# Three narrow chunks beside attention instead of five, with two attention steps to each d_ff tile from step 25

## The chip, the core and the metric

The kernel runs on one core of one Trainium2 chip. The metric is the device time of one execution in microseconds (us); lower is better. The profile is one execution on the same core, and its times are counted from the first instruction.

## What is computed

```python
def _attn_ref(q, k, v, omega):              # q, k, v: (4, 8, 576, 64); omega: (128, 64)
    scale = 1.0 / np.sqrt(np.sqrt(D))
    q_s, k_s = q * scale, k * scale
    def phi(x):
        proj = np.einsum('bhsd,md->bhsm', x, omega)
        h = proj - np.sum(x * x, axis=-1, keepdims=True) / 2.0
        return np.exp(h - np.max(h, axis=-1, keepdims=True)) / np.sqrt(m)
    q_p, k_p = phi(q_s), phi(k_s)
    kv = np.einsum('bhsm,bhsd->bhmd', k_p, v)
    z = np.sum(k_p, axis=2)
    num = np.einsum('bhsm,bhmd->bhsd', q_p, kv)
    den = np.einsum('bhsm,bhm->bhs', q_p, z)[..., None] + 1e-06
    return num / den

x = attention output as 2304 tokens x 512
h = x @ w_in                                # layer one: d_ff 2048
x = (np.maximum(h, 0) + alpha * np.minimum(h, 0)) @ w_out
out = ((x @ w_a) * (x @ w_b)) @ w_out2      # layer two: d_ff 1536
```

All values are fp32. Every fp32 product of the two layers is made of three faster ones: each operand is split into a high and a low part (`xh`/`xl`, `gh`/`gl`, and the two halves of a weight tile `w`), and high x high, high x low and low x high are summed.

## The kernel before

There are four stages. TensorE (PE) runs one fixed order of instructions; so does each other engine. Instructions stand in each engine's queue in the order in which the Python code issues them.

**Attention** goes in steps `s`, one token tile of one unit (a pair of heads, `u`) each. A step projects keys and queries (`pp(u, t)`, `a_proj`), takes the maxima (`nm`, VectorE, `a_max`) and exponentials (`ph`, ScalarE, up to 16 for two steps, `a_exp`). Later steps use the results: `kv` sums keys by values (`a_kv`), `tp` transposes the query features and copies them to `phT` (`a_t`; on ScalarE or VectorE, whichever the code counts as less loaded), `nd` multiplies by the kv state `kvp` and normalises (`rc`, `xn`, three VectorE instructions, `a_num`), and `xp` transposes the result into `xT` (`a_x`). `pp`, `tp`, `nd`, `xp` and the layer's input product `h` share one ring of five PSUM banks here, each reused after its readers are done.

**Layer one beside attention.** Layer one works by chunks of tokens and d_ff tiles `f`. A tile of a chunk is one input product `h` (12 matmuls), the activation (`u`, then a scalar-tensor-tensor, `gh`, `gl`) and one output product `y` (12 matmuls) that runs a while after it. A narrow chunk has 256 tokens. The first two narrow chunks go in two halves of the eight tiles; the first half's sums are parked in `xT` and added later (`xT<-y,xT`). Up to a point (`ALONE` pieces of `work0`) `A.run` takes one attention step with each tile. Behind it the `while` loop calls `group`, which takes two attention steps with two tiles, and leaves a group without tiles unless two are ready. In `group` the queue order is: `xp`, `kv`, `nd`, `nd`, `kv`, the late halves of the activation (`A.flush`), two projections with maxima and exponentials, x splits (`spread`), decoder work (`D_.go(5)`), `tp`, `y`, `tp`, `y`, then the `h` of the tiles.

**The decoder** unpacks weight tiles: `z` and `a` on GpSimd, `r` and `w` on ScalarE, a scalar-tensor-tensor `a`, an `ISA` instruction `a` on VectorE, and the low half of `w` on GpSimd or VectorE. It is paid by credit: `D_.step` gives it, 1 for a step and 2 for a group. There are 17 slots for tiles until attention is over.

**Layer one alone** works with wide chunks of 512 tokens (`Mlp.run`, class `Mlp` again), in two passes over d_ff: tiles 0 to 7 for all tokens that attention did not cover, then tiles 8 to 15 for all. `over` opens its buffers and splits the first inputs; `Mlp.open` takes its PSUM banks, four for outputs (`psy`) and four for inputs (`psh`). **Layer two** follows (`dual`, `back`) and is untouched.

The numbers that the change touches, before: `NCI = 5` narrow chunks, `REST = (512, 512)` wide ones in the first pass, `ALONE = 4` pieces run one step to a tile (16 tiles, steps 15 to 30).

Of the kernel before, what the change touches and what calls it, by code (L numbers as in the profile page):

```python
# [15 lines left out]
PSUM = bass.MemoryType.PSUM  # L16
# [7 lines left out]
KT = DM // P  # L24
# [8 lines left out]
WARM = 11  # L33
Q_LAG = 6
CI = 256
NCI = 5
NF0 = 8
NFH = 5
CB = 512
REST = (512, 512)  # L40
CHUNKS = (512, 512, 256, 512, 512)
NS = 25
NS1 = 17
# [9 lines left out]
DEC1 = 1.0  # L53
# [5 lines left out]
PACE2 = 1  # L59
PACE3 = 1  # L60
FIRST = 32
ALONE = 4
LAND = 5.0
SIDE = 0

# [2 lines left out]
def tile_kernel(ctx: ExitStack, tc: tile.TileContext, qT, kT, v1, omT, wbits, alpha, out):  # L68
# [37 lines left out]
    def place(q):  # L106

        if q < 20:
            return q
        if q < PB:  # L110
            return q if q < NS else q - NS
        return RING[(q - PB) % len(RING)]
# [14 lines left out]
    for ph in range(PH2):  # L127
        q = PB + QS * ph
        for j in range(2):
            f = 4 * ph + 2 * j  # L130
# [10 lines left out]
    def pick(*ways):  # L141

        def worst(w):
            return max(load[e] + w.get(e, 0.0) for e in load)

        i = min(range(len(ways)), key=lambda i: worst(ways[i]))
        for e, x in ways[i].items():
            load[e] += x
        return i
# [65 lines left out]
    class Decoder:  # L215
# [132 lines left out]
        def open(self, q):  # L348
            return place(q) in slots and (before[q] is None or self.free.get(before[q], False))
# [104 lines left out]
        def more(self, n):  # L454

            for _ in range(n):
                if self.advance() is not True:
                    return
# [11 lines left out]
    D_ = Decoder()  # L470
# [9 lines left out]
    class Mlp:  # L480
# [24 lines left out]
            self.banks = lambda h=None: self.open(pool, ybufs, h)  # L505

        def open(self, pool, ybufs, h):
            self.psy = pool(name=f"psy{self.cap}", bufs=ybufs, space=PSUM)
            self.psh, self.htag = h or (pool(name=f"psh{self.cap}", bufs=4, space=PSUM), "h")

        def split(self, ph, o, n, k):
            if (ph, o, k) in self.xs:
# [6 lines left out]

            way = pick({"dve": 1.2 * n / 1000}, *([] if self.pair or o == CI * NCI else [{"pool": 2.5 * n / 1000}]))  # L520
            (nc.vector, nc.gpsimd)[way].tensor_tensor(out=lo, in0=src, in1=hi.bitcast(F32), op=ALU.subtract)  # L521
# [466 lines left out]
    A = Mlp(st_m, CI, 2)  # L988
# [26 lines left out]
    with st_m:  # L1015
        A.banks((psp[0], "ps"))
        nxt_s = [SPLIT_AT]
        due = [0.0]

        def attn_next(high=None, low=None):  # L1020
            s = nxt_s[0]
            nxt_s[0] += 1
            D_.step(DEC1)
            pj = attn_1(s)
            if high:
                high()
            if pj:
                nm = a_max(*pj)
            loads(s)
            if low:  # L1030
                low()
            if pj:
                a_exp(*pj, nm)
            attn_2(s)
            A.after.append(lambda: attn_3(s))

        def attn_more():
            attn_next()
            A.flush()

        def inside(high, low):
            due[0] += 1.0
            if due[0] > 0 and nxt_s[0] < steps:
                due[0] -= 1.0
                attn_next(high, low)
            else:
                high()
                low()

        A.beside = inside  # L1050

        wait = {}

        def group(fronts, at):

            s = nxt_s[0]
            nxt_s[0] += 2
            D_.step(2 * DEC1)
            full = s < last_q
            todo = {n: wait[n][:2] for n in wait}  # L1060
            for n in wait:
                wait[n] = wait[n][2:]
            kv, t = list(todo["kv"]), list(todo["t"])
            for ut in todo["x"]:
                a_x(*ut)
            if kv:
                a_kv(*kv.pop(0))
            for ut in todo["num"]:
                a_num(*ut)
                wait["x"].append(ut)  # L1070
            if kv:
                a_kv(*kv.pop(0))
            spread(fronts, KT)
            A.flush()
            for x in (s, s + 1):
                pj = attn_1(x)
                loads(x)
                if pj:
                    a_exp(*pj, a_max(*pj))
                if x in ev["k"]:  # L1080
                    wait["kv"].append(ev["k"][x])
                if x in ev["q"]:
                    wait["t"].append(ev["q"][x])
            spread(line[at:at + 5], 2)
            D_.go(5)
            for i in range(2):
                if i < len(t):
                    a_t(*t[i])
                    wait["num"].append(t[i])
                if full:  # L1090
                    A.back_one(fronts, 2 - i)
            for w in fronts:
                A.whole(*w)
                if not full:
                    A.back_one(fronts)
            D_.go(3)

        def more():
            return nxt_s[0] < last_q or any(wait.values())

        def x_there(end, k, soon=False):
            b, t = divmod(end - 1, S)
            ut = (b * HG + k // 2, t // P)
            return ut in done["x"] or soon and ut in wait["x"][:2]

        def over():
            st_a.close()
            mlp_x.append(Mlp(st_u, CB, 4, RIGHT))
            for k in range(2):
                mlp_x[0].split(0, CI * NCI, CB, k)  # L1110


        work0 = [(0, CI * i, CI, fs, False) for fs in (range(NFH), range(NFH, NF0)) for i in range(2)]
        work0 += [(0, CI * i, CI, range(NF0), False) for i in range(2, NCI)]

        def ready(end, k):
            b, t = divmod(end - 1, S)
            while nxt_s[0] <= x_step[b * HG + k // 2, t // P]:
                due[0] -= 1
                attn_more()  # L1120

        def beside(ph, ci, i):
            A.flush()
            todo = [f for w in work0[ci:ci + 2] for f in w[3]]
            need = [2 * f for f in todo[i + 1:i + 2]] + [2 * todo[j] + 1 for j in (i - 1,) if j >= 0]
            while not all(q in D_.made for q in need) and nxt_s[0] < steps:
                due[0] -= 1
                attn_more()

        A.run(work0, beside, ready, stop=ALONE)  # L1130
        A.flush()
        started = [i for i in sorted(ev["k"]) if i < nxt_s[0]]
        wait.update({
            "kv": [ev["k"][i] for i in started if ev["k"][i] not in done["kv"]],
            "t": [ut for ut in queries if ut in phiq],
            "num": [ut for ut in queries if ut in phT],
            "x": [ut for ut in queries if ut in xns]})

        line = [(ph, o, n, f, lc) for ph, o, n, fs, lc in work0 for f in fs]

        def spread(fronts, most):

            todo = []
            for w in fronts:
                if w[:3] not in todo:
                    todo.append(w[:3])
            for ph, o, n in todo:
                for k in range(KT):
                    if most and (ph, o, k) not in A.xs and x_there(o + n, k):
                        A.split(ph, o, n, k)  # L1150
                        most -= 1

        i = sum(len(w[3]) for w in work0[:ALONE])
        while i < len(line):
            if not more():
                spread(line[i:i + 5], 2)
            pair = []
            early = 1 if more() else 0
            for w in line[i:i + 2]:
                ph, o, n, f, _ = w  # L1160
                if all((ph, o, k) in A.xs or x_there(o + n, k, True) for k in range(KT)) and D_.ready >= 2 * f + 2 - early:
                    pair.append(w)
            if len(pair) < 2 and more():
                pair = []
            if more():
                group(pair, i)
            else:
                for w in pair:
                    A.flush()
                    A.whole(*w)  # L1170
                    A.back_one(pair, 3)
                    D_.fill()
            i += len(pair)
        A.flush()
        while more():
            group([], i)
        over()
        while A.q:
            A.pop()
# [71 lines left out]
    with st_u:  # L1251
# [6 lines left out]
        work = []  # L1258
        for ph, fs, chunks in ((0, range(NF0), (CI,) * NCI + REST), (1, range(NF0, FA), CHUNKS)):
            work += [(ph, sum(chunks[:i]), n, fs, i == len(chunks) - 1)  # L1260
                     for i, n in enumerate(chunks) if ph or i >= NCI]

        def beside(ph, ci, i):
            D_.fetch()
            rate = RATE_A if ph == 0 else RATE_A2 if ci == len(REST) else RATE_X
            D_.step(rate * work[ci][2] / 384)
# [251 lines left out]
```

## Time and profile before

| what | value |
|---|---|
| median of 3 runs | 941.66 us (941.63 to 943.17) |
| the profiled execution's own time | 941.1 us |
| its span, first to last instruction | 939.3 us |
| TensorE matmul busy | 927.0 us, 99% |
| VectorE busy | 610.1 us, 65% |
| ScalarE busy | 508.9 us, 54% |
| GpSimd busy | 126.1 us, 13% |
| mean granted TensorE clock | 0.999 |

A timeline row gives the start, the length, the engine, the line, the operation with output and inputs, the shape and the count of merged instructions; in brackets how long the engine stood idle before it and who ended that. Instructions on one engine overlap by some tenths of a microsecond, so the distance from one start to the next is the better price of one. A busy engine says nothing of what it may be short of; the list of waits says who stood still for whom.

### The profile page before, as it was taken

What the parts mean: (1) busy time and instruction counts of PE and PEld (TensorE: products, weight loads), DVE (VectorE), ACT (ScalarE), POOL (GpSimd) and SP (SyncE); (2) the same over time, 40 slices, a digit from 0 to 9 for tenths busy, and PEclk for the clock granted to TensorE, in tenths of its full rate; (3) what the DMA queues carried; (4) which work ended last, traced back from release to release, by engine and by line L of the source; (5) the groups of instructions that cost most, each with busy time, mean ns of one, the idle gap of its engine ahead of it and who ended that gap; (6) DMA issues with size and microseconds to landing.
All of it is one profiled execution on the core that took longest, in us unless ns stands there. A gap on an engine that the chain in (4) does not pass through costs nothing.

```text
span 939.3 us, 16686 instructions
## 1 busy us (share of the span) xinstructions
PE 927.0 (99%) x6483; PEld 841.1 (90%) x6483; DVE 610.1 (65%) x1247; ACT 508.9 (54%) x1196; POOL 126.1 (13%) x107
## 2 busy tenths in 40 slices
PE   8899999999999999999999999999999999999998
PEld 7789999999888888889888999999999898989896
DVE  5987775644667677678676796866486833374633
ACT  7878766553455554455444555655456542444541
POOL 3677700000020201000000000000011111010201
PEclk9999999999999999999999999999999999999999
DMA  9454431000234342455555856169727368333323
GB/s 339 150 184 145 149 103 50 24 1 24 90 90 135 90 157 68 168 191 200 202 180 214 314 206 231 73 225 395 282 65 238 69 185 275 100 42 94 55 47 68
DMA packets 49566, 138.92 MB, mean 148 GB/s; under 512 B 4560, under 2 KB 11088, under 8 KB 49488
## 3 DMA queue, kind: packets, MB, share of 16 engines
q1 hardware_dynamic: 44592, 129.08, 38.6%
q0 software_dynamic: 4752, 8.65, 6.3%
q8 instruction: 51, 0.84, 0.4%
q14 instruction: 27, 0.22, 0.1%
q10 hardware_dynamic: 144, 0.13, 0.0%
HBM read 90.66 MB, written 47.19 MB: 147 GB/s over the span
## 4 chain that ended last, share of the span: by engine, by line
PE 94%; ACT 3%; DVE 2%; issue 0%; ACTq 0%
PE y L191 21%; PE h L191 21%; PE W L191 16%; PE o L191 16%; PE E L191 8%; PE B L191 4%; ACT ph L818 2%; PE tp L191 2%; PE kv L191 1%; PE nd L191 1%; PE xp L191 1%; DVE xl L521 0%; PE warm L191 0%; ACT r L259 0%; ACT phT L852 0%
## 5 line engine op out<-in xcount | busy, mean ns | idle before, releaser
L191 PE MATMUL h<-xh,w 128*128 128x256 f32 (+1 forms) x768 | 189.2, 338 | 1.1 <-DVE yo L191 0.7
L191 PE MATMUL y<-gh,w 128*128 128x256 f32 (+1 forms) x768 | 184.7, 339 | 0.0
L191 PEld LDWEIGHTS h<-xh,w 128*128 128x128 f32 x768 | 125.8, 190 | 16.8 <-DVE yo L191 0.9
L191 PEld LDWEIGHTS y<-gh,w 128*128 128x128 f32 x768 | 123.3, 189 | 15.0
L191 PE MATMUL o<-w,gh 128*128 128x512 f32 x432 | 133.2, 389 | 0.0
L191 PE MATMUL h<-xl,w 128*128 128x512 f32 (+1 forms) x384 | 109.9, 336 | 0.4 <-DVE xl L521 0.4
L191 PE MATMUL y<-gl,w 128*128 128x512 f32 (+1 forms) x384 | 109.5, 336 | 0.0
L191 PEld LDWEIGHTS o<-w,gh 128*128 128x128 f32 x432 | 81.0, 188 | 16.5
L191 DVE SCALAR_TENSOR_TENSOR h<-u,bend,h 128x512 f32<-128x512 f32 (+1 forms) x72 | 47.8, 664 | 56.5 <-ACT u L555 56.5
L191 PE MATMUL o<-w,gl 128*128 128x512 f32 x216 | 84.2, 390 | 0.0
L1417 POOL DMA_DIRECT2D out<-op x30 | 26.3, 875 | 421.9 <-ACT op L166 339.5
L567 ACT ACTIVATE gh<-h 128x512 fp32r<-128x512 f32 (+1 forms) x72 | 37.9, 527 | 64.3 <-DVE h L191 64.3
L191 PEld LDWEIGHTS h<-xl,w 128*128 128x128 f32 x384 | 64.4, 190 | 8.2 <-DVE xl L521 0.6
L191 PEld LDWEIGHTS y<-gl,w 128*128 128x128 f32 x384 | 64.1, 189 | 7.5
L555 ACT ACTIVATE u<-h 128x512 f32<-128x512 f32 (+1 forms) x72 | 38.0, 528 | 56.0 <-PE h L191 52.0
L521 POOL TENSOR_TENSOR xl<-xT,xh 128x512 fp32r<-128x512 f32 (+1 forms) x16 | 20.2, 1274 | 335.4 <-ACT xh L517 335.4
L166 ACT ACTIVATE u<-W 128x384 f32<-128x384 f32 x72 | 35.3, 492 | 50.6 <-PE W L191 46.8
L166 ACT ACTIVATE op<-o 128x512 f32<-128x512 f32 x51 | 30.4, 596 | 57.9 <-PE o L191 44.8
L191 DVE TENSOR_TENSOR u<-E,u 128x384 f32<-128x384 f32 x36 | 19.6, 555 | 52.5 <-PE E L191 49.7
L191 DVE TENSOR_TENSOR gl<-h,gh 128x512 fp32r<-128x512 f32 (+1 forms) x72 | 43.1, 598 | 15.4 <-ACT gh L567 14.6
L191 DVE CUSTOM_DVE_ANT_0 a<-a,r 128x1024 uint16<-128x1024 uint16 x68 | 48.9, 719 | 5.2 <-ACT r L259 1.2
L191 PEld LDWEIGHTS o<-w,gl 128*128 128x128 f32 x216 | 40.5, 188 | 8.4
(496 smaller groups left out, 1968.0 us busy)
## 6 DMA issues: line engine op xcount, KB each, us to landing
raw<-in_w SPq DMA_DIRECT2D x68, 512.0 KB, 4.8
w<-store SPq DMA_DIRECT2D x45, 512.0 KB, 6.7
store<-t_None SPq DMA_DIRECT2D x40, 512.0 KB, 3.6
st<-ypart SPq DMA_DIRECT2D x14, 768.0 KB, 7.7
out<-op POOLq DMA_DIRECT2D x30, 256.0 KB, 5.6
q<-in_qT SPq DMA_DIRECT2D x8, 576.0 KB, 4.1
v<-in_v SPq DMA_DIRECT2D x7, 650.0 KB, 5.6
yp<-ypart SPq DMA_DIRECT2D x4, 1024.0 KB, 5.8
```

The lines of the kernel that those rows point to most:

```text
L166: nc.scalar.activation(out, in_, AF.Copy)
L191: return call(*a, **k)
L521: (nc.vector, nc.gpsimd)[way].tensor_tensor(out=lo, in0=src, in1=hi.bitcast(F32), op=ALU.subtract)
L555: nc.scalar.activation(u_, hp, AF.Relu, scale=-1.0)
L567: nc.scalar.activation(gh, hp, AF.Copy)
L818: nc.scalar.activation(ph[:, 2 * pr + j], pair[j][:, o + pr], AF.Exp, bias=nm[:, j, o + pr:o + pr + 1])
L1417: nc.gpsimd.dma_start(out=dst, in_=op, accum_op=ALU.add)
```

## The change

- `NCI` 5 to 3 and `REST` from two to three wide chunks: tokens 768 to 1279 leave the narrow part and become one wide chunk.
- `ALONE` 4 to 2: one attention step with one tile ends after 10 tiles (steps 15 to 24). From step 25 on `group` runs.
- `group` now takes one tile, not two, with its two steps, one `y` at most between them, and the decoder gets 1 of credit for a group, not 2.
- `open` takes the input banks `psh` first, the output banks `psy` after them.
- `over` splits all four input quarters of the first wide chunk, not two.

```diff
-NCI = 5
+NCI = 3
-REST = (512, 512)
+REST = (512, 512, 512)
-ALONE = 4
+ALONE = 2
...
         def open(self, pool, ybufs, h):
+            self.psh, self.htag = h or (pool(name=f"psh{self.cap}", bufs=4, space=PSUM), "h")
             self.psy = pool(name=f"psy{self.cap}", bufs=ybufs, space=PSUM)
-            self.psh, self.htag = h or (pool(name=f"psh{self.cap}", bufs=4, space=PSUM), "h")
...
-            D_.step(2 * DEC1)
+            D_.step(DEC1)
...
                 if full:
-                    A.back_one(fronts, 2 - i)
+                    A.back_one(fronts, 1)
...
-            for k in range(2):
+            for k in range(KT):
                 mlp_x[0].split(0, CI * NCI, CB, k)
...
-            for w in line[i:i + 2]:
+            for w in line[i:i + 1] if more() else line[i:i + 2]:
...
-            if len(pair) < 2 and more():
-                pair = []
```

Three places show what this moves. The names are those of the steps above; the last number of a tile is the build's own and means nothing.

First place: TensorE at step 25, before.

```order
L191 MATMUL xp_2_1851<-ident,xn_2_1732 128x128 x2
L191 MATMUL h_0_5_1855<-xh_0_0_683,w_88 128x256
...
L191 MATMUL pp(5, 0)_False_1873<-xT,k_1381 128x128
...
L191 MATMUL kv_1505<-v_1070,ph_4_1792 64x65 x8
L191 MATMUL nd_4_1917<-kvp_170,phT_4_1837 64x65 x4
L191 MATMUL tp_2_1929<-ident,ph_2_1693 128x128 x4
...
L191 MATMUL xp_3_1948<-ident,xn_3_1830 128x128 x2
```

The same place on TensorE after the change:

```order
L191 MATMUL xp_2_1851<-ident,xn_2_1732 128x128 x2
L191 MATMUL xp_3_1855<-ident,xn_3_1830 128x128 x2
L191 MATMUL kv_1505<-v_1070,ph_4_1792 64x65 x8
L191 MATMUL nd_4_1868<-kvp_170,phT_4_1837 64x65 x4
L191 MATMUL pp(5, 0)_False_1878<-xT,k_1381 128x128
...
L191 MATMUL pp(5, 1)_False_1901<-xT,k_1381 128x128
```

The transpose `xp_3`, which stood behind `h`, `pp`, `kv`, `nd`, `tp` and a `y`, now stands directly behind `xp_2`.

Second place: ScalarE in the group of steps 29 and 30 of the changed kernel, from the second step's last exponentials.

```order
L818 ACTIVATE ph_0_2236<-pp(6, 0)_False_2222,nm(0, 6, 0)_2233 128x128 x2
L818 ACTIVATE ph_2_2237<-pp(6, 0)_False_2222,nm(0, 6, 0)_2233 128x128 x2
L517 ACTIVATE xh_512_0_2246<-xT 128x256
L517 ACTIVATE xh_512_1_2250<-xT 128x256
L259 ACTIVATE r_2258<-raw_2094 128x512
L308 ACTIVATE w_94<-a_2100 128x512
L852 ACTIVATE phT_1_2271<-tp_1_2266 128x512
L852 ACTIVATE phT_0_2290<-tp_0_2285 128x512
L587 ACTIVATE u_0_7_2305<-h_0_7_2292 128x256
L838 ACTIVATE kvp_170<-kv_1997 128x260
```

Before, `w_94` stood in step 27 on ScalarE, behind one step's exponentials and with no split ahead of it:

```order
L818 ACTIVATE ph_2_2091<-pp(5, 2)_False_2075,nm(0, 5, 2)_2085 128x128 x2
L818 ACTIVATE ph_1_2092<-pp(5, 2)_False_2075,nm(0, 5, 2)_2085 128x128 x2
L259 ACTIVATE r_2105<-raw_1995 128x512
L308 ACTIVATE w_94<-a_2001 128x512
L852 ACTIVATE phT_4_2138<-tp_4_2135 128x256
L894 ACTIVATE xT<-xp_2_2154 128x2x128
```

The last decoder tile now stands behind two steps' exponentials and two x splits, and both `phT` copies of the group stand behind it.

Third place: VectorE in the same group and the next of the changed kernel.

```order
L521 TENSOR_TENSOR xl_512_0_2247<-xT,xh_512_0_2246 128x256
L521 TENSOR_TENSOR xl_512_1_2251<-xT,xh_512_1_2250 128x256
L191 SCALAR_TENSOR_TENSOR a_2100<-z_2096,a_2100 128x512
L191 ISA a_2100<-a_2100,r_2098 128x1024
L191 SCALAR_TENSOR_TENSOR u_0_7_2305<-u_0_7_2305,bend,h_0_7_2292 128x256
...
L521 TENSOR_TENSOR xl_512_3_2416<-xT,xh_512_3_2415 128x256
L191 TENSOR_TENSOR xT<-y_0_0_2111,xT 128x256 x2
L191 TENSOR_TENSOR xT<-y_0_1_2112,xT 128x256 x2
L191 COPY phT_2_2448<-tp_2_2443 128x512
```

The decoder's `a` stands behind both `xl`, which read what ScalarE splits; one group on, `phT_2` stands behind two `xl` and four additions of the parked sums.

## Rows read from the trace of the kernel before

**Rows 1.** The page: busy time, share of the span, instructions of each engine.
```profile
PE 927.0 (99%) x6483; PEld 841.1 (90%) x6483; DVE 610.1 (65%) x1247; ACT 508.9 (54%) x1196; POOL 126.1 (13%) x107
```
**Rows 2.** Waits of TensorE: waiting <- waited for: us in total, times, longest.
```profile
PE h L191 <- DVE yo L191: 0.7, 1, 0.7
PE tp L191 <- DVE xn L191: 0.2, 1, 0.2
```
**Rows 3.** Chain of waits: start, us, engine and output, matmuls; narrow, then wide.
```profile
138.44 2.88 PE h L191 x24
...
252.51 2.72 PE h L191 x12
```
**Rows 4.** Timeline, TensorE: first transposes of steps 25, 31 and 39.
```profile
97.44 0.38 PE L191 MATMUL xp<-ident,xn 128*128 128x128 f32 x2
...
131.12 0.60 PE L191 MATMUL xp<-ident,xn 128*128 128x128 f32 x4
...
173.32 0.60 PE L191 MATMUL xp<-ident,xn 128*128 128x128 f32 x4
```
**Rows 5.** Timeline, all engines, at the end of the narrow chunks.
```profile
236.16 1.12 PE L191 MATMUL y<-gh,w 128*128 128x256 f32 x8
...
237.80 0.43 DVE L191 TENSOR_TENSOR gl<-u,gh 128x256 fp32r<-128x256 f32 x1 [0.48 <-ACT gh L594]
238.32 1.29 DVE L521 TENSOR_TENSOR xl<-xT,xh 128x512 fp32r<-128x512 f32 x2
...
241.33 0.50 PE L191 MATMUL h<-xh,w 128*128 128x512 f32 x1 [0.70 <-DVE yo L191]
```
**Rows 6.** Timeline, VectorE: the normalisation of step 24.
```profile
98.20 0.42 DVE L191 TENSOR_TENSOR xn<-nd,rc 128x256 f32<-128x256 f32 x1
```
**Rows 7.** Timeline, all engines: the group of steps 37 and 38.
```profile
163.11 0.48 DVE L191 SCALAR_TENSOR_TENSOR u<-u,bend,h 128x256 f32<-128x256 f32 x1 [0.96 <-ACT u L587]
...
165.87 0.61 PE L191 MATMUL pp(7, 3)_False<-xT,k 64*128 64x128 f32 x8
166.22 1.28 DVE L191 TENSOR_REDUCE nm(0, 7, 2)_3008<-pp(7, 2)_False 128x4 f32<-128x512 f32 x2
...
166.94 2.17 ACT L818 ACTIVATE ph<-pp(7, 2)_False,nm(0, 7, 2)_3008 128x128 f32<-128x128 f32 x8 [2.89 <-DVE nm(0, 7, 2)_3008 L191]
...
168.95 2.22 ACT L818 ACTIVATE ph<-pp(7, 3)_False,nm(0, 7, 3)_3031 128x128 f32<-128x128 f32 x8
...
170.94 0.83 ACT L517 ACTIVATE xh<-xT 128x256 fp32r<-128x256 f32 x2
...
171.50 0.76 DVE L521 TENSOR_TENSOR xl<-xT,xh 128x256 fp32r<-128x256 f32 x2 [2.81 <-ACT xh L517]
171.56 0.98 ACT L852 ACTIVATE phT<-tp 128x256 f32<-128x256 f32 x2
...
174.36 0.81 PE L191 MATMUL nd<-kvp,phT 128*64 128x65 f32 x22
```
**Rows 8.** Timeline, VectorE and ScalarE: decoder work and phT in single steps.
```profile
113.31 0.68 DVE L191 SCALAR_TENSOR_TENSOR a<-z,a 128x512 uint32<-128x512 uint32 x1
...
114.03 0.69 DVE L191 CUSTOM_DVE_ANT_0 a<-a,r 128x1024 uint16<-128x1024 uint16 x1
...
114.51 0.72 ACT L259 ACTIVATE r<-raw 128x512 uint32<-128x512 uint32 x1
...
115.07 0.68 ACT L308 ACTIVATE w<-a 128x512 fp32r<-128x512 f32 x1
...
115.59 0.43 ACT L852 ACTIVATE phT<-tp 128x256 f32<-128x256 f32 x1
```
**Rows 9.** Groups of instructions by shape, 97 to 131 us: additions of parked sums, decoder.
```profile
L191 DVE SCALAR_TENSOR_TENSOR a<-z,a 128x512 uint32<-128x512 uint32 x4 | 3.7, 930 | 0.0
...
L191 DVE TENSOR_TENSOR xT<-y,xT 128x256 f32<-128x256 f32 x4 | 1.4, 416 | 0.6 <-PE y L191 0.6
```
**Rows 10.** Windows: TensorE's busy time, instructions, granted clock, DMA share, GB/s.
```profile
18.00:20.00 2.00, 0.84 (x14) 1.00 1.08 404
```

## The prediction

> **What bounds the kernel now.** I read the page's busy times first: TensorE is busy for 927.0 of 939.3 us, every other engine at most 65% [rows 1]. A share that high is no proof, so next the waits of TensorE: beside the first 40 us there is one of 0.7 us where the wide chunks begin and one of 0.2 us in the grouped steps [rows 2]. So TensorE runs almost without a pause, and what the change is worth is the TensorE work that it takes away, less the pauses that it makes. For the first I read the chain, for the second the timelines of one group, of single steps and of the end of the narrow part.
>
> The profiled execution took 941.1 us, 0.6 under the median of the runs; the sum is made against 941.1. A measurement here can tell about 0.2% (1.9 us) from no change.
>
> **TensorE work taken away.** 512 tokens leave the narrow part. Two narrow products of 12 matmuls take 2.88 us, one wide one 2.72 [rows 3]. Eight tiles, each with an input and an output product: 16 x 0.16 = **2.6 us** less.
>
> Six steps (25 to 30) change from single steps to groups. From the transposes at 97.44 to those at 131.12 lie six single steps, 5.61 us each; less one `h` and one `y` (2.88) the attention in one is 2.73. From there to 173.32 lie four groups, 10.55 each; less two `h` and two `y` (5.76), halved, 2.39 [rows 3, 4]. 6 x 0.34 = **2.0 us** less: the same matmuls, with fewer changes between kinds. Steps differ a little in size, so 1.2 to 2.5.
>
> At the first wide product the wait of 0.7 us for `yo` goes [rows 2, 5]: with `psh` opened first, the banks that `yo` empties go to the outputs, needed three tiles later. What is late next? Only one `y` now lies between the last `h` and the last `y`. In the row before, the last `h` ends at 236.16 and `gl` at 238.23; with one `y` (1.44) in between, the late half is due near 238.56, its high half near 237.6, so at most 0.2 us is given back. The four splits follow `gl` at 0.65 each (1.29 for two [rows 5]) and end near 240.9; the fourth is due 2.2 us after 239.1, so it is hidden. Together **0.5 us** less.
>
> Gain: 2.6 + 2.0 + 0.5 = **5.1 us**. The rest of the kernel has the same work in the same order on TensorE; decoder work still ahead when attention ends is the same too (17 tiles made), with a wide chunk more to hide it.
>
> **Pauses that it makes.** A group keeps its two steps and loses one `h` and one `y`, its cover. I take the group at 162 to 173 us as a model, count from the end of the first projection (165.87) and subtract 2.88. TensorE reaches the next `xp` at 173.32, so 7.45 after, now **4.6**; the second `xp` 0.25 later, **4.8**; the first `nd` 1.04 after the first `xp` (174.36), now **5.6** [rows 4, 7].
>
> ScalarE must finish by then. From the maximum's start to the first exponential is 0.72; sixteen exponentials take 4.23 (166.94 to 171.17), fourteen about 3.7; the following operation starts 0.23 before the last one ends [rows 7]. With VectorE free the maxima start at about 0.1, so sixteen end at E = 5.05. The second `xp` takes the bank that the last exponentials leave, so it waits until E.
>
> I name the groups by steps and go through the seven heavy ones.
> - **25, 26.** `xp_3` stands right behind `xp_2`, due 97.6; its `xn` ended at 98.62 [rows 6], behind the decoder's operations of step 24, which stay where they are. Pause **1.1**.
> - **27, 28** (16 exponentials). E is past 4.8: 0.3. Behind the exponentials on ScalarE stand `r`, `w` (0.56 and 0.52 from start to start), then two `phT` (0.43 for half a tile, and 0.98 for half and whole) [rows 7, 8]. The first `phT` ends at E + 1.3 = 6.3, where `nd` is due at 5.9: 0.45; the second adds 0.25. Sum **1.0**.
> - **29, 30** (14). ScalarE's `u` stood behind `phT`, so VectorE gets to it late: scalar-tensor-tensor, copies, two normalisations and `gl` lie between it and the maxima, 3.1 us with two `gl` [rows 7], 2.7 with one. So the maxima start at 1.3 and E is 5.7; TensorE loses 0.9 to the banks. Now a chain through two engines: two `xh`, two `xl` (1.32 from the first `xh` to the last `xl` [rows 7]), scalar-tensor-tensor and `ISA` (1.4), `w` (0.6), `phT` (0.6) [rows 7, 8]. It starts at E - 0.23 and ends near 9.4; `nd` is due at 6.5: 2.9. The second `nd` needs the second `phT`, `u` and `kvp` behind it on ScalarE, three copies of some 0.45: 0.6 more. Sum **4.4**.
> - **31, 32** (14). Two `xh`, two `xl`, then four additions of the parked sums (1.4 [rows 9]) stand ahead of one `phT` on VectorE (0.6): done 3.1 after E, with `nd` due 1.3 after E and the first `nd` 0.1 late: 1.7; 0.4 for a bank. Sum **2.1**.
> - **33 to 38.** No decoder and no split: 0.6 (a bank, VectorE still behind), 0, and 0.5 for the sixteen of 37 and 38. Sum **1.1**. Groups after that have at most ten exponentials and pause no more than now.
>
> Pauses: 1.1 + 1.0 + 4.4 + 2.1 + 1.1 = **9.7 us**. Bounds: if VectorE is on time in each group, 6.8 remain (1.1, 0.9, 3.1, 1.5, 0.2); if the decoder's VectorE operation takes its mean of 0.93 [rows 9] rather than 0.68 and the delays add up, about 12.5. I take the middle, which follows the queues one group after another.
>
> DMA loads: keys, queries and values are issued in the same steps as before, now some 8 us for two steps rather than 11, still at least two steps ahead of their use; I cost them at nothing, and a late one would be seen as a wait of `pp` or `kv` for DMA.
>
> Sum: 941.1 - 5.1 + 9.7 = 945.7; the runs' median lay 0.6 above the profiled execution, so I take half of that: **946.0 us**, 0.46% above the median. With the bounds of pauses and gain 942.8 to 948.8.
>
> **The clock.** In the window 18 to 20 us TensorE was busy 0.84 of 2.00 us and the granted clock was 1.00 [rows 10]; by that row the pauses cost only their length. The Trainium skill ("TensorE: Matmul & The Clock Gate", section "HAM oscillation — how this bites in real kernels") says that idle gaps between bursts of matmuls make the gate throttle the array again, so that the next burst starts cold. By that rule the sum would be some 950; by the row it is 946. No single pause of the trace before is as long as the 2.9 us that I expect, so the row bears on it only in part.
>
> **Rivals.**
> - *The pauses stay under the gain: faster.* Place: the group of steps 29 and 30. If ScalarE and VectorE run ahead there, so that the exponentials end a good 2 us earlier than I put them, only step 25's 1.1 us, and some 1.5 elsewhere, remain. It decides where the pauses sum to less than 5.1 - 1.9 = 3.2. Then 941.1 - 5.1 + 2.6 = 938.6. For it: the grouped steps before paused 0.2 us in all. Against: the order of the queues, which no speed of VectorE shortens, since `phT` there stands behind seven operations that follow one another.
> - *Pauses and gain about equal.* The low bound of the pauses with the full gain gives 942.8; a little less, 941.7.
> - *The clock falls in a pause of steps 29 to 32.* 1.2 GHz instead of 2.4 doubles the matmuls; a group's TensorE work is some 7.8 us, and if half of one runs so, 4 us more: 950.
> - *The change doesn't do what it says* (groups that go without a tile). The order shows one tile in every group up to the last, so I give it nothing.
>
> **Chances.** Forecast 0.64; faster 0.09; equal 0.16; clock 0.11. The range leaves out the faster case and the far end of the clock case and takes in the bounds: 942.4 to 949.8. Within 0.2% (939.8 to 943.5) lie the equal case and the low edge of the forecast, less some of each: 0.16. Slower by over that 0.75, faster 0.09.
>
> **What would show it.** Right: waits of `xp` for VectorE near 98 us, of `nd` for ScalarE's `phT` between 110 and 140 us, the longest near 3 us; TensorE's narrow part over at about 203 us (before 241); the first wide `h` without a wait for `yo`; granted clock 1.00. Wrong: no `nd` wait over 1 us in that stretch; or waits for DMA; or a granted clock under 0.95 there; or new pauses in the wide part, which I hold to be none.

## The result and the profile after

The change makes the kernel slower: 948.03 us median of six runs (947.06 to 950.72) against 942.45 for the kernel before beside it (941.63 to 943.77). The ratio is 1.0071, 95% interval 1.0061 to 1.0081. The profiled execution took 949.5 us, its span 947.5.

The page of the changed kernel, busy times of the engines, against [rows 1]:

```profile
PE 928.4 (98%) x6291; PEld 832.3 (88%) x6291; DVE 605.9 (64%) x1220; ACT 506.1 (53%) x1173; POOL 133.5 (14%) x113
```

192 matmuls fewer (two narrow ones became one wide one), and yet TensorE is busy for 1.4 us longer, where the prediction took 4.6 us of its work away. So pauses need not be all of it: some of its work may have become slower.

Waits of TensorE from 97 to 206 us, the narrow part from step 25 on; before there were two, of 0.7 and 0.2 us [rows 2]:

```profile
PE nd L191 <- ACT phT L852: 2.8, 2, 2.5
PE nd L191 <- DVE phT L191: 1.3, 1, 1.3
PE xp L191 <- DVE xn L191: 0.9, 1, 0.9
PE xp L191 <- ACT ph L818: 0.4, 2, 0.3
PE nd L191 <- ACT kvp L838: 0.4, 1, 0.4
PE tp L191 <- DVE xn L191: 0.2, 1, 0.2
```

The timeline of TensorE shows where they stand (start, duration, operation, count, in brackets the idle time ahead and what ended it), with the first wide product as last row:

```profile
100.11 0.44 PE L191 MATMUL xp<-ident,xn 128*128 128x128 f32 x2 [0.86 <-DVE xn L191]
...
118.18 1.17 PE L191 MATMUL nd<-kvp,phT 128*64 128x65 f32 x24 [0.29 <-ACT phT L852]
...
126.17 0.44 PE L191 MATMUL xp<-ident,xn 128*128 128x128 f32 x2 [0.25 <-ACT ph L818]
...
129.74 0.69 PE L191 MATMUL nd<-kvp,phT 128*64 128x65 f32 x16 [2.52 <-ACT phT L852]
130.78 1.14 PE L191 MATMUL nd<-kvp,phT 128*64 128x65 f32 x16 [0.35 <-ACT kvp L838]
...
132.71 1.23 PE L191 MATMUL pp(6, 1)_False<-xT,k 64*128 64x128 f32 x8
...
142.22 0.69 PE L191 MATMUL nd<-kvp,phT 128*64 128x65 f32 x16 [1.34 <-DVE phT L191]
...
205.43 0.40 PE L191 MATMUL h<-xh,w 128*128 128x512 f32 x1
```

The waits come in the order and at the places that the prediction gave, the longest (2.52 us) for the `phT` that steps 29 and 30 make, which TensorE needs in the next group, ahead of the projections of steps 31 and 32. The first wide `h` waits for no `yo`, where before it did [rows 5]. The eight matmuls of `pp(6, 1)` at 132.71 take 1.23 us; eight such take 0.61 at full clock [rows 7]. The windows around them (length, TensorE's busy time, instructions, granted clock, DMA share, GB/s):

```profile
126.00:129.00 3.00, 1.05 (x18) 1.00 0.24 42
129.00:130.00 1.00, 0.26 (x8) 1.00 0.97 390
130.00:131.00 1.00, 0.65 (x20) 0.88 0.41 166
131.00:134.00 3.00, 3.00 (x44) 0.50 0.00 0
134.00:135.00 1.00, 1.00 (x20) 0.91 0.00 0
```

After 2.5 us without a matmul and another wait soon behind them, the clock goes from 2.4 to 1.2 GHz for some 3.4 us, in which TensorE was busy throughout. In 97 to 241 us of the kernel before the clock was 1.00.

ScalarE's timeline shows the queue that `phT` stood in, as the prediction described it:

```profile
123.90 2.21 ACT L818 ACTIVATE ph<-pp(6, 0)_False,nm(0, 6, 0)_2233 128x128 f32<-128x128 f32 x8
125.90 0.82 ACT L517 ACTIVATE xh<-xT 128x256 fp32r<-128x256 f32 x2
126.51 0.79 ACT L259 ACTIVATE r<-raw 128x512 uint32<-128x512 uint32 x1
128.57 0.63 ACT L308 ACTIVATE w<-a 128x512 fp32r<-128x512 f32 x1 [1.27 <-DVE a L191]
129.11 1.07 ACT L852 ACTIVATE phT<-tp 128x512 f32<-128x512 f32 x2
130.06 0.39 ACT L587 ACTIVATE u<-h 128x256 f32<-128x256 f32 x1
130.33 0.40 ACT L838 ACTIVATE kvp<-kv 128x260 f32<-128x260 f32 x1
```

`w` waits 1.27 us for VectorE's `a`, which stood behind `xl` there, and `phT` and `kvp` wait behind `w` without needing it.

**Balance of the two profiles.** From the transposes of step 25 to the first wide product: 143.89 us before, 106.55 after, 37.3 less. From there to the end of the span: 697.97 before, 742.07 after, 44.1 more. The start up to step 25, the same work in the same order on TensorE, took 97.44 and 98.88. It lay between 97.54 and 98.63 in the profiles of the runs below, and is not put down to the change.

### The profile page after: what moved, and what is told of

Its sections match the earlier page's. It is cut to its first block, busy times and chain, and to the rows that moved or that the text cites. A ratio compares the mean times of both kernels' runs of the same rounds, so it can differ in the third digit from the quotient of the medians.

```text
span 947.5 us, 16241 instructions
## 1 busy us (share of the span) xinstructions
PE 928.4 (98%) x6291; PEld 832.3 (88%) x6291; DVE 605.9 (64%) x1220; ACT 506.1 (53%) x1173; POOL 133.5 (14%) x113
## 3 DMA queue, kind: packets, MB, share of 16 engines
q0 software_dynamic: 4752, 8.65, 6.3%
## 4 chain that ended last, share of the span: by engine, by line
PE 90%; ACT 5%; DVE 4%; DMA 1%; issue 1%; SPq 0%; ACTq 0%
PE h L191 20%; PE y L191 20%; PE W L191 16%; PE o L191 16%; PE E L191 8%; PE B L191 4%; ACT ph L818 3%; PE nd L191 1%; PE kv L191 1%; PE tp L191 1%; PE xp L191 1%; DMA v<-in_v 1%; DVE a L191 1%; DVE xl L521 1%; ACT phT L852 0%
## 5 line engine op out<-in xcount | busy, mean ns | idle before, releaser
L191 PE MATMUL h<-xh,w 128*128 128x512 f32 (+1 forms) x704 | 191.0, 353 | 0.5 <-DVE gl L191 0.4
L191 PE MATMUL y<-gh,w 128*128 128x512 f32 (+1 forms) x704 | 187.0, 353 | 0.1
L191 PEld LDWEIGHTS h<-xh,w 128*128 128x128 f32 x704 | 120.6, 189 | 19.2 <-DVE gl L191 0.6
L191 PEld LDWEIGHTS y<-gh,w 128*128 128x128 f32 x704 | 119.0, 189 | 17.7 <-ACT gh L594 0.3
L191 DVE SCALAR_TENSOR_TENSOR h<-u,bend,h 128x512 f32<-128x512 f32 (+1 forms) x74 | 50.9, 688 | 69.2 <-ACT u L555 69.2
L567 ACT ACTIVATE gh<-h 128x512 fp32r<-128x512 f32 (+1 forms) x74 | 40.5, 547 | 66.4 <-DVE h L191 66.4
L521 POOL TENSOR_TENSOR xl<-xT,xh 128x512 fp32r<-128x512 f32 (+1 forms) x22 | 28.0, 1284 | 322.2 <-ACT xh L517 322.2
L191 PEld LDWEIGHTS h<-xl,w 128*128 128x128 f32 x352 | 61.5, 189 | 9.4 <-DVE xl L521 0.6
L191 PEld LDWEIGHTS y<-gl,w 128*128 128x128 f32 x352 | 61.3, 189 | 9.3 <-DVE gl L191 0.6
L191 DVE TENSOR_TENSOR gl<-h,gh 128x512 fp32r<-128x512 f32 (+1 forms) x74 | 46.1, 623 | 20.9 <-ACT gh L567 20.0
```

The source lines that it names most:

```text
L191: return call(*a, **k)
L567: nc.scalar.activation(gh, hp, AF.Copy)
```

## The experiments

Each was timed in four to eleven executions beside the kernel before on the same chip (medians 941.45 to 941.58). The theory is that the queues in front of `phT` and `kvp` make the pauses, and that the clock adds to them. The main rivals: ScalarE and VectorE have simply too much to do for groups of 8 us, or the cost lies outside the pauses.

| run | median us | ratio to before (95%) |
|---|---|---|
| the changed kernel again | 948.24 | 1.007 (1.0058 to 1.0083) |
| `phT` first | 947.31 | 1.0056 (1.0043 to 1.0068) |
| filling behind the wait | 950.27 | 1.0089 (1.0075 to 1.0102) |
| filling ahead of the wait | 947.76 | 1.0063 (1.005 to 1.0077) |
| before, in groups from step 25 | 951.25 | 1.0097 (1.0082 to 1.0112) |
| before, banks and splits | 940.34 | 0.9986 (0.9977 to 0.9995) |
| changed, five narrow chunks | 949.95 | 1.0087 (1.0073 to 1.01) |
| `phT` first, `kvp` ahead | 943.60 | 1.0024 (1.0015 to 1.0032) |
| the same, `kv` first | 944.02 | 1.0026 (1.0017 to 1.0035) |
| the same, single steps to 27 | 943.51 | 1.0024 (1.0015 to 1.0032) |
| changed, single steps to 30 | 944.60 | 1.0025 (1.0014 to 1.0036) |

### The changed kernel again

> The changed kernel as it is, as the yardstick for the others of this row of runs: 5 to 6 us above the kernel before, as in the result. If the fall of the granted clock near 131 us is part of the cost, it is there again, at the same place; if it was an accident of one execution, it is not.

As expected: 948.24, the same waits (2.52, 1.33 and 0.86 us the longest), and the clock at 0.50 from 131 to 134 us again. It belongs to the change.

### phT ahead of the splits and the decoder

```diff
             ...
-            spread(line[at:at + 5], 2)
-            D_.go(5)
             for i in range(2):
                 ...
                     A.back_one(fronts, 1)
+            spread(line[at:at + 5], 2)
+            D_.go(5)
```

> The changed kernel with one move in a group: the x splits and the decoder's work are issued behind the transposes of the two steps and not ahead of them, so that phT stands ahead of xh, xl and the parked-sum additions in the queues of ScalarE and VectorE. Theory (order of the queues): the nd waits for phT of 2.5 and 1.3 us go, the clock stays at 1.00, and 5 to 6 us come back against the changed kernel: about 942 to 943, equal to the kernel before. Rival (ScalarE and VectorE simply have too much to do for groups of 8 us, in whatever order): phT comes earlier but the next group's maxima and exponentials come later by as much, xp waits grow by 2 to 3 us, and at most 2 us come back. Other rival: the x splits come too late and the first wide product waits for xh or xl.

Only 0.9 us came back, not 5 to 6. TensorE's timeline of this kernel:

```profile
126.30 0.64 PE L191 MATMUL nd<-kvp,phT 128*64 128x65 f32 x16
129.98 1.14 PE L191 MATMUL nd<-kvp,phT 128*64 128x65 f32 x16 [3.05 <-ACT kvp L838]
```

The first `nd` has its `phT` at once, as the theory had it, but the second needs `kvp`, and that copy now stands where `phT` stood. ScalarE:

```profile
125.63 0.83 ACT L517 ACTIVATE xh<-xT 128x256 fp32r<-128x256 f32 x2
126.24 0.80 ACT L259 ACTIVATE r<-raw 128x512 uint32<-128x512 uint32 x1
128.31 0.63 ACT L308 ACTIVATE w<-a 128x512 fp32r<-128x512 f32 x1 [1.27 <-DVE a L191]
128.84 0.37 ACT L587 ACTIVATE u<-h 128x256 f32<-128x256 f32 x1
129.11 0.54 ACT L894 ACTIVATE xT<-xp 128x128 f32<-128x128 f32 x2
129.53 0.40 ACT L838 ACTIVATE kvp<-kv 128x260 f32<-128x260 f32 x1
```

The pause moved from one item of the queue to the next and grew to 3.05 us, and the clock fell again (0.50 from 130 to 133 us). The 1.3 us of the next group did go. I had looked at `phT` alone and not at who is last when it is early.

### kvp brought ahead too

```diff
-            spread(line[at:at + 5], 2)
-            D_.go(5)
+            if s >= SPLIT_AT + 18:
+                spread(line[at:at + 5], 2)
+            if s != SPLIT_AT + 14:
+                D_.go(5)
```

`SPLIT_AT` is 15 and `s` the group's first step.

> The kernel of the experiment that put phT first, and further: the x splits start two groups later, and the decoder's work of the group of steps 29 and 30 is left to the next group, so that kvp no longer stands behind two xh, r and a w that waits for VectorE. Theory (what costs is the queue in front of kvp on ScalarE): the nd wait of 3.05 us falls to about 1, with it the fall of the granted clock after it goes, and 3 to 4 us come back against that kernel: 943 to 944. Rival: the wait moves on once more, to a w that now comes late or to the maxima: less than 1.5 us back. Clock's rival: the wait shrinks but the clock falls as before: 2 us back.

943.60, inside what the theory gave. TensorE and ScalarE in the same group:

```profile
127.34 0.69 PE L191 MATMUL nd<-kvp,phT 128*64 128x65 f32 x16 [0.55 <-ACT kvp L838]
```

```profile
125.00 0.70 ACT L852 ACTIVATE phT<-tp 128x512 f32<-128x512 f32 x1
125.48 0.50 ACT L587 ACTIVATE u<-h 128x256 f32<-128x256 f32 x1
125.75 0.82 ACT L259 ACTIVATE r<-raw 128x512 uint32<-128x512 uint32 x1
126.34 0.67 ACT L894 ACTIVATE xT<-xp 128x128 f32<-128x128 f32 x2
126.76 0.53 ACT L838 ACTIVATE kvp<-kv 128x260 f32<-128x260 f32 x1
```

The same exponentials on the same engine and the same order on TensorE, and the wait falls from 3.05 to 0.55 us; the clock is 1.00 in the whole narrow part from step 25 on. ScalarE does as much in sum (busy for 505.9 us, 506.1 in the changed kernel), but two `xh` and a `w` that waits for VectorE now stand in later groups. So what stood ahead of `phT` and `kvp` made the long pause, not the amount of ScalarE's work over the whole part. Whether the group could have held all of it in another order was not run. 4.6 us of the changed kernel's 6.7 come back so, with the wait for the next group's `phT` and the fall of the clock among them. 2.1 stay.

### Two fillings, for the price of the clock

The first put 20 matmuls of the warm-up tile, discarded afterwards, into the bank of the first `nd`; the second does the transposes of one `xp` ten times over, ahead of `kv`. Both stand in the group that begins with step 31, where the wait is.

```diff
         nb = bank(f"nd{u}_{t}")
+        for _ in range(fill):
+            tensor.matmul(nb[:, :256], lhsT=warm[:, :P], rhs=warm, start=True, stop=True)
...
+                a_num(*ut, fill=20 if s == SPLIT_AT + 16 and k == 0 else 0)
```

> The changed kernel with 20 matmuls of the warm-up tile added between kv and the first nd of the group of steps 29 and 30, where TensorE paused 2.5 us; their result is overwritten. They take about 2.2 us at full clock and fill the pause. If the fall of the granted clock after the pause costs what the records say (3.3 us at 1.2 GHz, so some 1.6 us), the clock stays at 1.00 from 129 to 136 us and the time falls by 1.3 to 1.7 us against the changed kernel. If the clock's fall is hidden by other waits (the next phT is late anyway), the clock stays up and the time stays within 0.5 us. If the pause is not what lowers the clock, it falls all the same.

```diff
-            for a in range(2):
+            for a in times * (0, 1):
                 tensor.transpose(xp[:, a, :], xn[:, a], ident)
...
+                a_x(*ut, times=10 if s == SPLIT_AT + 16 and ut[1] < 4 else 1)
```

> The changed kernel with the transposes of one xp in the group of steps 29 and 30 done ten times over instead of once (18 transposes more, same bank, same result). They stand in front of kv and wait for nothing, so that TensorE works through 2.3 of the 2.5 us in which it paused for phT; the first run with a filling put it behind that wait. phT, kvp and all that stands behind them come no sooner, so the pause itself cannot be won. Theory (the fall of the granted clock after the pause costs 1.6 us by itself): the clock stays at 1.00 from 129 to 136 us and the time falls by 1.2 to 1.7 us against the changed kernel, 946.5 to 947. Rival (the fall costs nothing, since what follows waits anyway): the clock stays up and the time stays within 0.5 us of 948.2. Other rival (it is not the pause that lowers the clock): it falls as before, and the time is the same.

The first missed its place. The filling itself waited 2.52 us for the copy of `phT`, though it does not read it: `nd` takes over a bank that this copy empties. It then lengthened the way, and the time rose by 2.0 us. The second, windows as above:

```profile
126.00:129.00 3.00, 2.94 (x36) 1.00 0.02 5
129.00:130.00 1.00, 0.51 (x16) 1.00 0.21 36
130.00:131.00 1.00, 0.65 (x22) 1.00 0.74 172
131.00:134.00 3.00, 3.00 (x58) 1.00 0.40 158
```

`nd` starts 4.10 us after the group's first `xp`, as without the filling (4.07), so nothing else moved. The clock stays at 1.00, and from this `nd` to the next `tp` it takes 3.88 us (129.50 to 133.38) and not 5.44 (129.41 to 134.85 in the changed kernel run beside the first experiments): in this pair of profiles the fall costs 1.56 us. The narrow part was 1.36 us shorter in them (105.15 against 106.51). The medians differ by 0.5 only (947.76 and 948.24) with intervals that overlap: less than the 1.2 to 1.7 expected, and within what the rival allowed. So the clock stays up when the pause is filled, and the size of its cost is not confirmed by the times. Executions of one kernel at different mean granted clocks speak for a cost, though a mean does not tell where the clock fell: with `phT` first, 945.21 at 1.000 and 947.20 to 947.91 at 0.996 to 0.998; with five narrow chunks, 948.65 at 1.000 and 949.83 to 951.05 at 0.998.

### The kernel before, in groups from step 25

```diff
-ALONE = 4
+ALONE = 2
```

> The kernel before with one part alone: the attention steps go in groups from step 25 and not from 31, each group with two tiles of d_ff as before. The prediction's term: 2.0 us less TensorE work for the six steps, less up to 1.1 us of xp_3's wait for its xn, so 0.9 to 2.0 us faster than the kernel before. Rival: the difference between single and grouped steps came from the size of the steps and the pauses inside them and not from the grouping: within 0.5 us of the kernel before, or slower by the wait of xp_3.

9.7 us slower, where I expected 1 to 2 faster. With two tiles in each group TensorE has more work to hide things with, and still:

```profile
123.13 0.44 PE L191 MATMUL xp<-ident,xn 128*128 128x128 f32 x2 [1.54 <-ACT phT L852]
...
133.23 2.08 PE L191 MATMUL y<-gh,w 128*128 128x256 f32 x8 [3.43 <-DVE xT L191]
```

VectorE in front of that `y`:

```profile
131.75 0.76 DVE L521 TENSOR_TENSOR xl<-xT,xh 128x256 fp32r<-128x256 f32 x2 [2.43 <-ACT xh L517]
132.43 1.41 DVE L191 TENSOR_TENSOR xT<-y,xT 128x256 f32<-128x256 f32 x4
```

The additions of the parked sums, which free `y`'s banks, stand behind `xl`, `xl` behind `xh`, and `xh` on ScalarE behind all sixteen exponentials of two steps. TensorE stands for 3.4 us and then runs at 0.50 from 133 to 139. So grouping steps 25 to 30, beside the decoder and the splits, costs by itself, with two tiles in a group as with one, though the longest wait is another one here.

### Banks and splits alone

```diff
-            self.psy = pool(name=f"psy{self.cap}", bufs=ybufs, space=PSUM)
             ...
+            self.psy = pool(name=f"psy{self.cap}", bufs=ybufs, space=PSUM)
...
-            for k in range(2):
+            for k in range(KT):
```

> The kernel before with two parts alone: the input banks opened first, and all four x splits of the first wide chunk ahead of it. Theory: the wait of 0.7 us for yo at the first wide product goes and nothing takes its place: 0.5 to 0.7 us faster than before. Rival: the first wide y waits for a bank as long, or xl comes too late: no change within 0.2 us.

1.1 us faster than before (median), somewhat more than expected; the interval, 0.05% to 0.23%, excludes no change. The first wide `h` starts at 240.78 without a wait, directly behind the last `y`, and the narrow part from step 25 takes 143.04 us and not 143.89. Of all the kernels run this is the fastest.

### Five narrow chunks

```diff
-NCI = 3
-REST = (512, 512, 512)
+NCI = 5
+REST = (512, 512)
```

> The changed kernel with five narrow chunks as before, so that everything else of the change stands (groups of one tile from step 25, banks, splits) and 16 more tiles of the narrow form are worked off behind attention. By the prediction's price, 16 pairs of narrow products cost 2.6 us more than the 16 wide products of a chunk: 950.8 us, with the same pauses at the same groups. By the trace after, in which the stretch behind the narrow part grew by 44.1 us where 43.5 were priced, 2.0 us more: 950.2. Rival: the narrow products were the dearer by less still, or the pauses need the shorter row of tiles: at most 949.

949.95: the waits are the same to 0.01 us (2.52, 1.33, 0.86), and 16 wide products in place of 32 narrow ones are worth 1.7 us, not 2.6; the profiles agree (45.8 us more in the narrow part, 44.1 less behind it). Behind the narrow part it has 697.96 us, as the kernel before; so a wide chunk costs 44.1 us, 2.76 for each of its 16 products, where the chain's row shows 2.72 [rows 3]. The trace shows where some of that lies: the first wide `y` of the changed kernel takes 3.04 us (213.62 to 216.66) and 2.72 with five narrow chunks, since its second matmul starts only once `gl` is written.

### Single steps up to 30, or up to 27

```diff
-ALONE = 2
+ALONE = 4
```

> The changed kernel with one part undone: single steps up to step 30, as before, and groups only from step 31, still with one tile each and three narrow chunks. Theory (the pauses come from the decoder's work and the splits beside groups of one tile at steps 25 to 32): the waits of xp for xn, of nd for phT and the clock's fall go up to 131 us, some 4 to 6 us come back, but three groups late in the narrow part have no tile and pause 1 to 2 us each: 942 to 945. Rival: the groups of 31 to 38 pause as much as before without the decoder, since ScalarE has to do sixteen exponentials in 8 us: no better than 947. Other rival: no pause takes their place and it beats the kernel before: 939 to 941.

944.60: the waits up to 131 us are gone, as expected, and the price is at the end, where three groups have no tile:

```profile
194.64 0.41 PE L191 MATMUL xp<-ident,xn 128*128 128x128 f32 x2 [1.29 <-DVE rc L191]
195.38 0.43 PE L191 MATMUL xp<-ident,xn 128*128 128x128 f32 x2 [0.33 <-DVE xn L191]
...
197.23 0.47 PE L191 MATMUL xp<-ident,xn 128*128 128x128 f32 x1 [0.79 <-DVE xn L191]
```

2.4 us of waits, and the clock at 0.50 from 196 to 202 us, into the first wide products. Executions in which the mean granted clock was 1.000 took 943.13 and 943.22.

The two last runs tried to win the rest, both from the kernel with `kvp` ahead: first `kv` in front of `xp`, then besides that single steps up to 27.

```diff
+            if kv:
+                a_kv(*kv.pop(0))
             for ut in todo["x"]:
                 a_x(*ut)
-            if kv:
-                a_kv(*kv.pop(0))
```

> The kernel of the experiment before that brought kvp ahead, and in each group the first kv in front of the xp instead of behind them. Theory (xp_3 of step 25 waits 1.0 us for its xn because nothing lies between it and xp_2): the 16 matmuls of a kv, 0.57 us, cover as much of that wait, and the waits of xp for a bank of the exponentials, 0.4 us in sum, become waits of kv for the same exponentials: 0.5 to 0.6 us faster than that kernel, 943.0. Rival: nd, now right behind xp and nearer to phT, waits as much as xp waits less: no change.

```diff
-ALONE = 2
+ALONE = 3
```

> The kernel of the run beside this one (phT first, x splits late, kv ahead of xp), and single steps up to step 27 and not 24: one and a half groups fewer, so that the last groups of the narrow part still have their tiles. Theory: of the changed kernel's cost, the pauses of steps 25 to 28 (xp_3 and the first phT, about 1.5 us) and the small losses of the groups of one tile (0.4 us each) go, and the 1.7 us that the wide chunk is cheaper and the 1.1 us of the banks and splits stay: 940.5 to 942, equal to the kernel before. Rival: the groups now begin on even steps, so that the decoder's work and kvp fall together in another group and a wait of 2 to 3 us with a fall of the clock comes back: 944 to 946.

Both missed. With `kv` first the wait for `xn` falls from 0.98 to 0.25 us, and the narrow part is no shorter for it (102.35 us against 101.99). The trace shows why: the new order is dearer by itself. For the same matmuls, from a group's first operation to its projections, the last run takes 2.52 us (`kv` at 149.89 to `pp` at 152.41) and the changed kernel 2.31 (`xp` at 149.01 to `pp` at 151.32), and the `h` ahead of it takes 0.09 more: 0.3 us in a group.

With single steps up to 27 the waits that the view lists for the narrow part sum to 1.5 us, and it takes 100.72 us. What follows takes 742.8 and not 742.1 as in the changed kernel: the first wide `h` now waits for `xl` (8.65 us to the next product, not 8.19), and the first wide `y` longer for `gl` (3.34 us, not 3.04). This run is still 2 us slower than the kernel before, but it holds the dearer order and these waits, so what the change is worth without its pauses is not shown by a run.

## Why the prediction was right, and where not

Direction and range held (942.4 to 949.8, measured 948.0); the time itself was 2 us too low. One of the prediction's own signs of being wrong came all the same: the granted clock fell to 0.50 where it was to stay at 1.00. Step by step:

- **The pauses, 9.7.** Right in place, order and kind, and nearly right in size. The brackets of the timeline sum to 6.0 us, but the forecast counted from start to start, and counted so a wait costs more. Here are the same two operations, before and after:

```profile
131.65 0.69 PE L191 MATMUL kv<-v,ph 128*64 128x65 f32 x16
132.16 0.64 PE L191 MATMUL nd<-kvp,phT 128*64 128x65 f32 x16
```

```profile
126.53 0.69 PE L191 MATMUL kv<-v,ph 128*64 128x65 f32 x16
129.74 0.69 PE L191 MATMUL nd<-kvp,phT 128*64 128x65 f32 x16 [2.52 <-ACT phT L852]
```

From `kv` to `nd` it is 0.51 us before and 3.21 after: 2.70 lost, with 2.52 in the bracket. The other bracketed waits cost 0.2 to 0.3 more than their brackets too. Short waits get no bracket here at all: from `tp` at 146.98 to `h` it is 0.49 us, and 0.14 at 184.90. With every distance set against the same operations without a wait, 1.1 was forecast for `xp_3` and 1.07 lost; 1.0 for steps 27 and 28, 1.13 lost (0.36, 0.47, 0.30); 4.4 for 29 and 30 (0.9, 2.9 and 0.6), 3.8 lost (0.47, 2.70, and 0.62 as in the second filling, where the clock stayed up); 2.1 for 31 and 32, 1.9 lost (1.58 and 0.35); 1.1 for the rest, 0.5 lost. That is 8.5 us, and 9.1 with three short waits that were not forecast. The chain through ScalarE and VectorE was sized well. The waits for banks were sized too large: I put the end of the exponentials too late.
- **Narrow to wide, 2.6.** Mis-sized: 1.7 by the runs with five and three narrow chunks, 2.0 by the balance of the profiles. I took 2.72 us for a wide product from one row; over a whole chunk it is 2.76, and 0.3 of the 0.6 us that this makes is the first wide `y`'s wait.
- **Six steps in groups, 2.0.** About 1.2 came, at the low end of the 1.2 to 2.5 forecast. This is an estimate, what the balance leaves: the narrow part is 37.3 us shorter; the 32 products (46.1) and the wait for `yo` (0.6) taken away, the pauses (9.1) and the clock (1.5) added, would make it 36.1 shorter. It is not that the groups now have one tile. A group without a wait takes the same for attention as before:

```profile
151.70 0.60 PE L191 MATMUL xp<-ident,xn 128*128 128x128 f32 x4
...
162.44 0.49 PE L191 MATMUL xp<-ident,xn 128*128 128x128 f32 x3
```

```profile
149.01 0.60 PE L191 MATMUL xp<-ident,xn 128*128 128x128 f32 x4
...
156.87 0.49 PE L191 MATMUL xp<-ident,xn 128*128 128x128 f32 x3
```

Before, 10.74 us less the 5.76 of two tiles; after, 7.86 less the 2.88 of one: 4.98 both times.
- **The wait for `yo` and the splits, 0.5.** Right: 0.6 in the changed kernel's profile, and 1.1 by the medians of the run with these two parts alone. As forecast, 0.2 us is given back, at the last narrow `y` (203.89).
- **The clock.** I put its fall at nothing in the sum, gave it a chance of 0.11 and leaned on [rows 10], where a stretch of 2 us with TensorE busy for 0.84 left it at 1.00. It fell in each profile of the changed kernel. The Trainium skill ("TensorE: Matmul & The Clock Gate", section "HAM oscillation — how this bites in real kernels") names the mechanism: after an idle gap between bursts the next burst starts cold. The trace agrees in part: the clock was at 0.50 from 131 to 134 us, but the first `nd` behind the pause still had 1.00 (129 to 130 us). The size was nearer to 1.5 us than to the 4 of the rival. The row that I set against it came from the start of the kernel and showed no pause as long as the one that I forecast, as the prediction itself said.
- **DMA and the wide part.** No wait for a load from 97 us on, as costed. Behind the narrow part I held that there would be no new pause, and there is a small one, 0.3 us at the first wide `y`.

So by the profiles the clock is most of what the sum lacked, 1.5 of the 2 us; by the medians of the second filling it is 0.5. The rest is what is left of errors that partly cancelled, which is luck: pauses 0.6 too large, against 0.6 on the products and 0.7 on the grouping. Without pauses and clock the change would have won some 3.9 us by this account, an estimate (2.0, 1.2 and 0.6), and not 5.1.

## What to carry to other kernels

When an engine's queue holds something that waits for another engine, all that stands behind it waits too; bringing one item ahead only makes the next one late, so ask before the edit who needs each item behind the waiting one. A wait costs more than the idle time in its bracket, so set starts against starts before calling a forecast of it wrong: here 9.1 us against 6.0. And a pause of some 2.5 us in a busy TensorE may have to be priced with the time at 1.2 GHz that follows it, here 1.56 us on 2.52 in a pair of profiles.

## What the runs showed of the chip that I had not expected

- The granted clock fell with TensorE standing: with `phT` first it was 0.81 between 129 and 130 us, where TensorE was busy 0.02 us. In the first filling's profiled execution a pause of 2.52 us, followed by 2.6 us of matmuls without a gap, left it at 1.00 (three other executions of that kernel had a mean of 0.996 to 0.998; where it fell there is not recorded). So the length of one pause did not decide it alone in these two profiles.
- In the profile of the changed kernel run again the clock also fell near the start (0.50 from 22 to 24 us), in work that the change does not touch, and in the first profile it did not. So the mean granted clock of an execution does not tell by itself where the clock fell.
